# Low parts of split weights a tick later, the last weight pair two ticks later, and other ticks for the scores of the second unit, in an attention and gated feed-forward kernel

## Chip, cores and metric

The kernel runs on one core of one Trainium2 chip. The metric is device time in microseconds for one execution. Three runs of the kernel before took 1147.52, 1148.4 and 1149.6 us, with a median of 1148.4. A change of 0.2% is 2.3 us.

## What is computed

The reference does attention over 8 batches, 8 heads, 576 positions and 64 dimensions, with a window of 32 keys (heads 0 to 3) or of 128 keys of which every fourth counts (heads 4 to 7), and then a gated feed-forward layer over the 4608 resulting rows of 512 numbers:

```python
scores = scale * np.matmul(q, k.transpose(0, 1, 3, 2))
scores = np.where(masks[None], scores, -1e9)
attn = np.exp(scores - np.max(scores, axis=-1, keepdims=True))
attn = attn / (np.sum(attn, axis=-1, keepdims=True) + 1e-09)
x = (attn @ v).transpose(0, 2, 1, 3).reshape(B * S, H * D)
xn = x / np.sqrt(np.mean(x * x, axis=-1, keepdims=True) + 1e-06) * rms_g
g = xn @ w_gate
out = (g * (1 / (1 + np.exp(-g))) * (xn @ w_val)) @ w_out
```

Weights are 512 x 1536 (gate, value) and 1536 x 512 (output). They come as float64, as two 32-bit words each, and the kernel turns them into float32 itself.

## The kernel before

**Units and parts.** The rows are worked off in 16 units u of 288 rows (half a batch). A unit's attention has 14 bursts (a block of queries of two heads): each needs scores (q), four or five ticks later transposes of the normalised probabilities (t), and then outputs (o). A unit's feed-forward has 12 column blocks j of 128, each in three parts: gate (part 0), val (part 1) and proj (part 2, the output product of the block before). TensorE (PE) runs these products; the attention of unit u + 1 is woven into the feed-forward of unit u.

**Ticks.** The order of work is written out by hand in ticks. `now[0]` counts them. 25 ticks come before the main loop (attention of unit 0); then each part of each block is a tick t = 3(uN + j) + part, with N = 12 blocks (loop at L790 to L815; t = 2 is the first, as the gate and val of block 0 stand at the end of the first loop). In a tick PE gets its 8 or 12 matmuls and then, by `attend` (L752), the transposes, outputs and scores that fall into it. What the other engines have to do is put off: `later(dt, rank, fn)` (L110) files a function for the tick dt ahead, and `flush` (L113) at the start of a tick issues what is filed for it, in order of rank. Each engine works off its own queue in the order of issue, so the rank is the place in the queue. Ranks of one tick: 0 tanh on ScalarE (ACT) or prod on VectorE (V, L679), 0.2 emptying the transposes (ACT L446, from unit 2 on also V L448), 0.5 emptying outputs and splitting h (ACT L690, GpSimd (POOL) L691), 0.6 normalising x (L585, L602, L603), 0.7 the score maximum (V L361, L366), 0.8 silu (V L666), 0.9 the low part of a query (V L344), 2 the exponentials (ACT L376), -1 or 2.1 the sums and the normalisation (V L385 and L386, POOL L391 or ACT L389), 3 to 3.3 high parts of keys, queries and values (ACT), 4 adding outputs (V L421), 5 a step of weight decoding (V) or the low part of keys (POOL L335), 5.1 the low part of values (POOL L305), 6 splitting a weight, 8 to 9 the next rebase, 9.9 the next weight load (SP).

**Weights.** 36 pieces (a block of gate, val or output weights) make 18 pairs. A pair is loaded raw, rebased on ACT (`rebase`, L151, with a multiply on POOL at L162) and then decoded on V: for the pairs from the fifth on in two steps, `rest` (L176) and `whole` (L180). `step` (L208) takes the next of these from a list; if the pair is not rebased yet, it first calls `ahead` (L217), which rebases. In the main loop of unit 0 one step is filed per tick (L797); the last pair, with the output blocks 10 and 11, has its steps in ticks 31 and 32 and its rebase in tick 31. Unit 0 multiplies in full float32; from unit 1 on (t = 36) each product is made of three matmuls with high and low parts. For that, `split_weight` (L227) takes one piece per tick: at even ticks from 4 to 30, and at every tick from 37 on (L794). ACT copies the high part (L242) and V or POOL subtracts it to get the low part (L243), both at rank 6 of the same tick; POOL does it at even ticks from 38 on.

**The plan of unit 1.** `plan` (L745) files the bursts of a unit in ticks. For unit 1 the ticks are given as a list (L767), relative to t = 0; transposes follow after 5 and outputs after 7 ticks.

**Banks.** Gate and val products alternate between the PSUM banks "g" and "v": `bank` (L634) gives block j's gate and val the two in turn. Transposes in a gate or val tick go into unused columns of that tick's own bank; in a proj tick they get a tile of their own in the bank `bank("g", j)` (L812). Scores use the single bank "s" from tick 4 on (L814).

```python
                if used and (t >= SPLITS[2] or t % 2 == 0 and SPLITS[0] <= t < SPLITS[1]):
                    later(0, 6, lambda: split_weight(*used.pop(0), V if t < SPLITS[1] or t % 2 else G))
                if u == 0:
                    decode(1)
```

Of the kernel before, what the change touches and what calls it, by code (L numbers as in the profile page):

```python
# [14 lines left out]
ALU = mybir.AluOpType  # L15
# [24 lines left out]
SIGNS = 4  # L40
SPLITS = 4, 31, 37


ORDER = [(0, 0, "q"), (0, 1, "q"), (0, 0, "v"), (0, 2, "q"), (0, 0, "w"), (0, 1, "v"), (0, 3, "qv"), (0, 2, "v"),
         (0, 0, "g"), (0, 0, "w"), (0, 0, "w"), (1, 0, "qv")]
# [22 lines left out]
def attn_moe(ctx: ExitStack, tc: tile.TileContext, qk_in, v_in, w_gate, w_val, w_out, rms_g, outT):  # L68
# [41 lines left out]
    def later(dt, rank, fn):  # L110
        put_off.setdefault(now[0] + dt, []).append((rank, fn))

    def flush():  # L113
        for _, fn in sorted(put_off.pop(now[0], []), key=lambda e: e[0]):
            fn()
# [86 lines left out]
    def decode(k):  # L202

        for i in range(k):
            later(0, 5 + 2 * i, step)
        later(0, 8.9, rebase_next)
# [16 lines left out]
    def single(kind, j):  # L223
        n = pieces.index((kind, j))
        return fs[n // 2][:, n % 2]

    def split_weight(kind, j, e):  # L227
        n = pieces.index((kind, j))
        m, k = divmod(n, 2)

        tag = f"hi{n if n % 4 == 3 and n < 2 * NP - 4 else n - n % 4}"
        if tag not in his:
            parts = 1 if n % 4 == 3 and n < 2 * NP - 4 else 3 if n < 2 * NP - 4 else 4
            his[tag] = cst.tile([P, parts, NC, P], F32R, tag=tag, name=f"{tag}_{kind}{j}")
        hi = his[tag][:, 0 if tag == f"hi{n}" else n % 4]
        if k == 0:
            los[m] = cst.tile([P, 2, NC, P], F32R, tag=f"slot{state['free']}", name=f"lo_{m}")
        else:
            state["free"] = m
        lo = los[m][:, k]  # L240
        wts[kind, j] = hi, lo
        A.copy(out=hi, in_=single(kind, j))  # L242
        e.tensor_tensor(out=lo, in0=single(kind, j), in1=hi, op=ALU.subtract)  # L243


    heads, vs, late = {}, {}, []
# [387 lines left out]
    def bank(kind, j):  # L634
        return "gv"[(j + (kind == "v")) % 2]
# [62 lines left out]
    def proj(u, j):  # L698
        if u == 0:
            used.append(("o", j))  # L700
        h = hs.pop((u, j))
        for d in range(NC):
            if j == 0:
                acc[u, d] = ps.tile([P, 512], F32, tag=f"acc{d}", name=f"acc_{u}_{d}")[:, :U]
            three(acc[u, d], weight("o", u, j), d, h, j == 0, j == NJ - 1)
            if j == NJ - 1:
                later(1, 0.7, lambda d=d: give(u, d))
# [37 lines left out]
    def plan(u, base, q_at, t_at, o_at):  # L745
        for b, *ts in zip(bursts(u), q_at, t_at, o_at):
            for kind, t in zip("qto", ts):
                events.setdefault(base + t, {})[kind] = b
        events.setdefault(base + o_at[-1] + (4 if u == 1 else 3), {})["sum"] = u
        events.setdefault(base + o_at[-1] + (4, 7, 5)[min(u, 2)], {})["apply"] = u  # L750
# [12 lines left out]
    for u in range(1, NU):  # L763
        q_at = [LAST - (LAST - EARLY[u > NNAT]) * (nb - 1 - k) // (nb - 1) for k in range(nb)]
        t_at, o_at = [t + 5 for t in q_at], [t + 8 for t in q_at]
        if u < NNAT:
            q_at = (-4, -2, -1, 1, 2, 4, 5, 7, 8, 10, 11, 13, 14, 16)  # L767
            t_at, o_at = [t + 5 for t in q_at], [t + 7 for t in q_at]
        plan(u, ends - 2 + 3 * NJ * (u - 1), q_at, t_at, o_at)
    for n in range(ends):  # L770
# [19 lines left out]
    for u in range(NU):  # L790
        for j in range(NJ):
            for part in range(0 if u + j else 2, 3):
                t = 3 * (u * NJ + j) + part
                if used and (t >= SPLITS[2] or t % 2 == 0 and SPLITS[0] <= t < SPLITS[1]):  # L794
                    later(0, 6, lambda: split_weight(*used.pop(0), V if t < SPLITS[1] or t % 2 else G))
                if u == 0:
                    decode(1)  # L797
                opening = len(ops) <= 2
                flush()
                if opening and not late:  # L800
                    early.close()
                    late.append(ctx.enter_context(tc.tile_pool(name="late", bufs=2)))
                if part == 0:
                    free = gate(u, j)
                elif part == 1:
                    free = val(u, j)
                else:
                    if prev is not None:
                        proj(*prev)
                    prev = (u, j)  # L810
                    free = None
                    if "t" in events.get(now[0], {}):  # L812
                        free = ps.tile([P, 512], F32, tag=bank("g", j), name=f"t_{u}_{j}")[:, :2 * QB]
                attend(free, s_tag="acc2" if t < 4 else "s")  # L814
                now[0] += 1  # L815
# [70 lines left out]
```

## Time and profile before

| | |
|---|---|
| median of three runs | 1148.4 us |
| the profiled execution: its own time | 1148.22 us |
| its span, from the first to the last instruction | 1146.4 us |
| mean granted clock of TensorE, share of 2.4 GHz | 0.997 |
| PE busy | 1120.8 us, 98% of the span |
| V, ACT, POOL busy | 69%, 62%, 54% |
| DMA | 82.19 MB, 72 GB/s on average |

Times in the trace are microseconds from the start of the span. Engines are PE (TensorE matmuls), PEld (its weight loads), DVE (VectorE, called V in the text), ACT (ScalarE), POOL (GpSimd), SP (the queue that issues DMAs). A timeline row gives start, duration, engine, line, operation, what is written and read, how many instructions were merged (x8), and in brackets the idle time of the engine just before, with the instruction whose end released it. Since matmuls are pipelined, their durations overlap. The profile is of one execution, so sums are made against 1148.22.

### The profile page before, as it was taken

How to read it: one execution, taken by the hardware profiler on the slowest of the kernel's cores; microseconds unless marked ns; L12 is line 12 of the kernel's file. 1: busy time of each engine (PE TensorE's matmuls, PEld its weight loads, DVE VectorE, ACT ScalarE, POOL GpSimd, SP SyncE). 2: the span in 40 equal slices, each digit the busy share in tenths (PEclk: the TensorE clock that was granted, in tenths of full speed). 3: DMA queues.
4: the chain of work that ended last, by engine and by line, in shares of the span. 5: the costliest groups of instructions: out<-in, count | busy, mean ns of one | idle time of the engine just before them, and what ended most of it. 6: DMA issues, size and time to landing. Idle time of an engine off the chain costs nothing.

```text
span 1146.4 us, 25956 instructions
## 1 busy us (share of the span) xinstructions
PE 1120.8 (98%) x8357; PEld 1088.0 (95%) x8357; DVE 793.4 (69%) x2893; ACT 714.6 (62%) x2610; POOL 620.8 (54%) x1073
## 2 busy tenths in 40 slices
PE   8898888999999999999999999999999999999998
PEld 7676778999999999999999999999999999999998
DVE  7889865867767586776758677585866758586411
ACT  5686676766657576675757657576765757576311
POOL 8235576655546465564547556465655646565211
PEclk9999999999999999999999999999999999999999
DMA  9555211311212121121212213121221312120000
GB/s 246 168 202 205 89 48 38 93 50 50 83 38 82 40 84 52 52 89 33 79 41 83 58 41 94 34 86 41 71 63 45 95 27 87 41 79 15 2 21 21
DMA packets 61545, 82.19 MB, mean 72 GB/s; under 512 B 7298, under 2 KB 41090, under 8 KB 61410
## 3 DMA queue, kind: packets, MB, share of 16 engines
q1 hardware_dynamic: 61410, 80.54, 23.6%
q8 instruction: 67, 1.10, 0.4%
q14 instruction: 68, 0.56, 0.2%
HBM read 71.08 MB, written 9.44 MB: 70 GB/s over the span
## 4 chain that ended last, share of the span: by engine, by line
PE 85%; DVE 6%; ACT 4%; issue 2%; DMA 1%; POOL 1%; POOLq 0%; SPq 0%; DVEq 0%; ACTq 0%
PE acc L622 8%; PE g L622 8%; PE v L622 8%; PE acc L623 8%; PE g L624 8%; PE g L623 8%; PE acc L624 8%; PE v L623 8%; PE v L624 8%; PE s L489 3%; PE o L477 3%; PE o L478 1%; PE busy L739 1%; ACT t L376 1%; DVE lo L243 1%
## 5 line engine op out<-in xcount | busy, mean ns | idle before, releaser
L691 POOL TENSOR_TENSOR hlo<-th,hhi 128x288 fp32r<-128x288 f32 x180 | 145.2, 807 | 201.5 <-ACT hhi L690 153.7
L624 PE MATMUL acc<-hhi,lo 128*128 128x288 f32 x720 | 212.2, 295 | 0.0
L391 POOL TENSOR_SCALAR t<-t,sum 72x72 f32<-72x72 f32 (+3 forms) x414 | 154.0, 384 | 71.9 <-DVE sum L386 65.2
L624 PE MATMUL v<-xhi,lo 128*128 128x288 f32 x612 | 180.8, 295 | 0.0
L624 PE MATMUL g<-xhi,lo 128*128 128x288 f32 x612 | 180.6, 295 | 0.0
L376 ACT ACTIVATE t<-t,sum 96x128 f32<-96x128 f32 (+3 forms) x448 | 165.6, 375 | 11.7 <-DVE sum L366 11.0
L690 ACT CAST hhi<-th 128x288 fp32r<-128x288 f32 x180 | 78.1, 434 | 141.0 <-DVE th L679 138.8
L305 POOL TENSOR_TENSOR vlo<-vt,vhi 128x128 fp32r<-128x128 f32 x196 | 93.3, 476 | 109.3 <-ACT vhi L301 96.9
L421 DVE TENSOR_TENSOR xraw<-o,xraw 64x96 f32<-64x96 f32 (+1 forms) x392 | 106.8, 272 | 56.4 <-ACT xraw L411 50.4
L661 ACT ACTIVATE th<-g 128x288 f32<-128x288 f32 x180 | 73.9, 410 | 106.6 <-PE g L624 87.7
L624 PEld LDWEIGHTS acc<-hhi,lo 128*128 128x128 f32 x720 | 135.6, 188 | 0.0
L666 DVE SCALAR_TENSOR_TENSOR th<-th,g 128x288 f32<-128x288 f32 x180 | 80.4, 447 | 69.4 <-ACT th L661 69.4
L624 PEld LDWEIGHTS v<-xhi,lo 128*128 128x128 f32 x612 | 115.3, 188 | 0.0
L624 PEld LDWEIGHTS g<-xhi,lo 128*128 128x128 f32 x612 | 115.0, 188 | 0.0
L622 PE MATMUL g<-xhi,hi_g 128*128 128x288 f32 x357 | 110.7, 310 | 1.6 <-DVE sum L385 0.9
L335 POOL TENSOR_TENSOR ks<-qk,ks 128x288 fp32r<-128x288 f32 (+2 forms) x112 | 111.0, 1005 | 0.0
L622 PE MATMUL acc<-hhi,hi_o 128*128 128x288 f32 x360 | 110.8, 308 | 0.0
L411 ACT COPY xraw<-o 64x96 f32<-64x96 f32 (+1 forms) x392 | 101.5, 259 | 12.5 <-PE o L478 10.1
L679 DVE TENSOR_TENSOR th<-th,v 128x288 f32<-128x288 f32 x180 | 81.5, 453 | 38.1 <-PE v L624 30.0
L623 PE MATMUL acc<-hlo,hi_o 128*128 128x288 f32 x360 | 106.9, 297 | 0.0
L361 DVE TENSOR_TENSOR t<-s,mask 96x256 f32<-96x256 f32 (+3 forms) x196 | 71.5, 365 | 50.9 <-PE s L489 45.7
L623 PE MATMUL g<-xlo,hi_g 128*128 128x288 f32 x322 | 94.8, 294 | 0.0
(184 smaller groups left out, 3581.2 us busy)
## 6 DMA issues: line engine op xcount, KB each, us to landing
qk<-in_qk_dram SPq DMA_DIRECT2D x60, 288.0 KB, 2.8
vt<-in_v_dram SPq DMA_DIRECT2D x196, 64.0 KB, 1.9
qk<-in_qk_dram SPq DMA_DIRECT2D x30, 352.0 KB, 3.0
out_dram<-ot SPq DMA_DIRECT2D x64, 144.0 KB, 1.9
qk<-in_qk_dram SPq DMA_DIRECT2D x30, 304.0 KB, 2.8
raw<-in_w_gate_dram SPq DMA_DIRECT2D x12, 512.0 KB, 4.7
raw<-in_w_val_dram SPq DMA_DIRECT2D x12, 512.0 KB, 5.3
raw<-in_w_out_dram SPq DMA_DIRECT2D x12, 512.0 KB, 4.3
```

Source lines behind the costliest of these rows:

```text
L305: G.tensor_tensor(out=vl, in0=vs.pop(b), in1=vh, op=ALU.subtract)
L335: ek.tensor_tensor(out=ks[:, 1, :nkt], in0=kr, in1=ks[:, 0, :nkt], op=ALU.subtract)
L376: A.activation(out=t[:nq, a, :n], in_=t[:nq, a, :n], func=AF.Exp, scale=-1.0, bias=sm[:nq, a, 0:1], accum_out=sm[:nq, a, 1:2] if u else None)
L391: (V if u == 0 and (c, i) > (NC - 1, 0) else G).tensor_scalar(out=t[:nq, a, :n], in0=t[:nq, a, :n], scalar1=sm[:nq, a, 3:4], scalar2=1.0, ...
L411: A.copy(out=to[a * D:(a + 1) * D], in_=o[a * D:(a + 1) * D, (2 + a) * nq:(3 + a) * nq])
L421: V.tensor_tensor(out=to[rows], in0=o[rows, a * nq:(a + 1) * nq], in1=to[rows], op=ALU.add)
L622: PE.matmul(out, wh[:, cc, :], xh, start=start, stop=False)
L623: PE.matmul(out, wh[:, cc, :], xl, start=False, stop=False)
L624: PE.matmul(out, wl[:, cc, :], xh, start=False, stop=stop)
L666: V.scalar_tensor_tensor(out=t, in0=t, scalar=1.0, in1=g, op0=ALU.add, op1=ALU.mult)
L679: V.tensor_tensor(out=t, in0=t, in1=v_ps[:, :U], op=ALU.mult)
L691: G.tensor_tensor(out=lo, in0=t, in1=hi, op=ALU.subtract)
```

## The change

Three things change. The low part of a split weight is filed one tick later, at rank 3.4, instead of being issued right behind its high part. In ticks 31 and 32 no decode step is filed; at the end of tick 32 (rank 8.9) the rebase of the last pair is filed, and its two steps fall into ticks 33 and 34. The scores of unit 1 that were at ticks 5, 8, 11 and 14 go to 6, 9, 12 and 15, with the transposes five and the outputs seven ticks behind them.

```diff
--- before.py
+++ after.py
@@ -40,6 +40,7 @@
 SIGNS = 4
 SPLITS = 4, 31, 37
 
+PAUSE = 31, 32
 
@@ -240,7 +241,7 @@
         lo = los[m][:, k]
         wts[kind, j] = hi, lo
         A.copy(out=hi, in_=single(kind, j))
-        e.tensor_tensor(out=lo, in0=single(kind, j), in1=hi, op=ALU.subtract)
+        later(1, 3.4, lambda: e.tensor_tensor(out=lo, in0=single(kind, j), in1=hi, op=ALU.subtract))
 
@@ -764,7 +765,7 @@
         q_at = [LAST - (LAST - EARLY[u > NNAT]) * (nb - 1 - k) // (nb - 1) for k in range(nb)]
         t_at, o_at = [t + 5 for t in q_at], [t + 8 for t in q_at]
         if u < NNAT:
-            q_at = (-4, -2, -1, 1, 2, 4, 5, 7, 8, 10, 11, 13, 14, 16)
+            q_at = (-4, -2, -1, 1, 2, 4, 6, 7, 9, 10, 12, 13, 15, 16)
             t_at, o_at = [t + 5 for t in q_at], [t + 7 for t in q_at]
         plan(u, ends - 2 + 3 * NJ * (u - 1), q_at, t_at, o_at)
@@ -794,7 +795,9 @@
                 if used and (t >= SPLITS[2] or t % 2 == 0 and SPLITS[0] <= t < SPLITS[1]):
                     later(0, 6, lambda: split_weight(*used.pop(0), V if t < SPLITS[1] or t % 2 else G))
                 if u == 0:
-                    decode(1)
+                    decode(t not in PAUSE)
+                    if t == PAUSE[-1]:
+                        later(0, 8.9, ahead)
                 opening = len(ops) <= 2
                 flush()
                 if opening and not late:
```

## Rows read from the trace of the kernel before

**Rows 1.** Stretches: start:end, length, busy us of each engine (instructions), PEclk, DMA share, GB/s

```profile
36.00:88.00 52.00, 48.08 (x247) 38.21 (x246) 43.71 (x126) 42.05 (x134) 14.42 (x10) 0.97 0.52 183
88.00:130.00 42.00, 37.02 (x162) 27.70 (x160) 39.17 (x61) 23.75 (x60) 22.01 (x20) 1.00 0.44 154
130.00:190.00 60.00, 50.62 (x364) 48.13 (x364) 42.69 (x160) 43.58 (x152) 42.80 (x64) 0.97 0.21 60
190.00:1146.40 956.40, 952.18 (x7406) 948.20 (x7404) 641.79 (x2426) 583.42 (x2189) 513.27 (x918) 1.00 0.19 56
```

**Rows 2.** Timeline of PE, ticks 5, 6 and 8

```profile
48.54 0.49 PE L472 MATMUL o<-pt,v 128*128 128x192 f32 x2
51.85 0.58 PE L486 MATMUL s<-qk 128*72 128x104 f32 x4 [2.83 <-DVE sum L366]
52.27 3.81 PE L619 MATMUL g<-xn,f 128*128 128x288 f32 x8
...
58.90 2.13 PE L619 MATMUL acc<-h,f 128*128 128x288 f32 x8
```

**Rows 3.** Stretches of 2 us, columns as in rows 1

```profile
52.00:54.00 2.00, 2.00 (x8) 1.56 (x8) 2.00 (x7) 1.84 (x4) 0.00 (x0) 0.58 0.96 389
...
148.00:150.00 2.00, 2.00 (x12) 1.98 (x11) 0.89 (x4) 1.67 (x6) 2.00 (x4) 0.50 0.04 8
150.00:152.00 2.00, 2.00 (x13) 2.00 (x12) 1.58 (x4) 0.81 (x3) 1.07 (x3) 0.67 0.00 1
```

**Rows 4.** Timeline of DVE, end of tick 4 and start of tick 5

```profile
48.59 1.29 DVE L172 SCALAR_TENSOR_TENSOR f<-raw,f 128x1024 uint32<-128x1024 uint32 x1
50.33 0.69 DVE L243 TENSOR_TENSOR lo<-f,hi_g 128x512 fp32r<-128x512 f32 x1 [0.45 <-ACT hi_g L242]
50.94 0.45 DVE L679 TENSOR_TENSOR h<-h,v 128x288 f32<-128x288 f32 x1
```

**Rows 5.** Timeline of ACT, the same place

```profile
49.70 0.60 ACT L242 CAST hi_g<-f 128x512 fp32r<-128x512 f32 x1
51.42 0.32 ACT L446 COPY pt<-v 128x192 f32<-128x192 f32 x1 [1.12 <-DVE h L679]
```

**Rows 6.** Timeline of PE, ticks 18 to 57: rows with idle time, and proj(10)

```profile
84.17 2.21 PE L619 MATMUL g<-xn,f 128*128 128x288 f32 x8 [0.50 <-ACT pt L446]
...
99.13 2.21 PE L619 MATMUL g<-xn,f 128*128 128x288 f32 x8 [0.44 <-DVE h L679]
...
106.74 2.21 PE L619 MATMUL g<-xn,f 128*128 128x288 f32 x8 [1.52 <-DVE h L679]
...
113.86 2.21 PE L619 MATMUL g<-xn,f 128*128 128x288 f32 x8 [0.50 <-DVE h L679]
...
122.24 2.21 PE L619 MATMUL g<-xn,f 128*128 128x288 f32 x8 [1.23 <-DVE h L679]
...
126.84 2.10 PE L619 MATMUL acc<-h,f 128*128 128x288 f32 x8
...
129.79 0.37 PE L622 MATMUL g<-xhi,hi_g 128*128 128x288 f32 x1 [0.68 <-ACT pt L446]
...
147.04 0.40 PE L622 MATMUL v<-xhi,hi_o 128*128 128x288 f32 x1 [1.78 <-DVE pt L448]
...
183.58 0.37 PE L622 MATMUL g<-xhi,hi_g 128*128 128x288 f32 x1 [0.86 <-DVE sum L385]
```

**Rows 7.** Timeline of DVE, ticks 22, 31, 35 and 41

```profile
97.41 1.29 DVE L243 TENSOR_TENSOR lo<-f,hi_g 128x512 fp32r<-128x512 f32 x1
...
120.02 1.80 DVE L177 SCALAR_TENSOR_TENSOR raw<-raw 128x1024 uint32<-128x1024 uint32 x1 [0.82 <-POOL raw L162]
...
129.24 0.45 DVE L679 TENSOR_TENSOR h<-h,v 128x288 f32<-128x288 f32 x1
...
145.64 0.69 DVE L243 TENSOR_TENSOR lo<-f,hi_o 128x512 fp32r<-128x512 f32 x1 [1.16 <-POOL vlo L305]
```

**Rows 8.** Timeline of POOL, while V made a low part at 97.41

```profile
96.38 1.78 POOL L335 TENSOR_TENSOR ks<-qk,ks 128x288 fp32r<-128x288 f32 x1
```

## The prediction

> **What bounds the kernel now.** I read the stretch table first, then the PE timeline with its idle times, then the VectorE (V) and ScalarE (ACT) timelines before each idle time. "Tick t" is step 3j+part of the main loop; the change touches ticks 4 to 59.
>
> The stretch table [rows 1] says where time can be had. From 190 us to the end PE is busy 952.18 of 956.40 us: nothing is left there, so whatever is gained or lost before 190 us arrives at the end unchanged, for PE simply starts its full stretch earlier or later. Before that, PE leaves 52.00 - 48.08 = 3.9 us (36 to 88), 42.00 - 37.02 = 5.0 us (88 to 130) and 60.00 - 50.62 = 9.4 us (130 to 190) idle, and the granted clock is 0.97 in the first and the last of these. V is busy 39.17 of 42.00 us between 88 and 130: there it is nearly as full as it can be.
>
> The largest single hole is at tick 5 [rows 2]. PE finishes the outputs behind proj(0) at 49.03 (48.54 + 0.49) and waits 2.83 us for V's score maximum before it may write tick 5's scores at 51.85, because ticks 4 and 5 share the one bank "s". Then the gate matmuls of tick 6 take 3.81 us where the same eight took 2.13 at tick 8: the granted clock is 0.58 from 52 to 54 [rows 3], so they ran mostly at 1.2 GHz instead of 2.4, after PE had stood still.
>
> V's timeline tells why the maximum is late [rows 4]. The sign step of tick 4 ends at 49.88. Then comes tick 4's low part (L243), which cannot start before ScalarE has made the high part, at 49.70 + 0.60 = 50.30 [rows 5]; V stands 0.45 us, subtracts for 0.69, and only then runs prod(1) (L679, 50.94) and the maximum. ACT in turn waits for prod(1) before it empties the transposes at 51.42. So a result that PE needs 14 ticks later (piece n is split at tick 23+n and used at 37+n, for n from 14) stands ahead of work that PE needs at once.
>
> **The change part by part.**
>
> 1. *Low parts a tick later, rank 3.4.* Nothing is added or removed: 14 low parts on V (even ticks 4 to 30), 11 on V and 11 on POOL (ticks 37 to 58). Each now stands behind the next tick's prod, maximum, silu and query low part, on POOL also behind the normalisation and hlo, and ahead of that tick's add and decode step. Its high part is then long done, so the wait for ACT goes too; no DMA hangs on it.
>
> At tick 5: sign ends 49.88, prod(1) takes 0.45 and ends about 50.3; ACT, free of the high part at 50.30, copies the transposes in 0.32, to 50.6; gate(2) can start at 50.7, against 52.27. That is 1.57 us, less 0.42 for the score matmuls that now come at tick 6 (52.27 - 51.85): **1.15**. The clock price of that hole is 3.81 - 2.13 = 1.68. What is left of the hole is 50.7 - 49.03 = 1.67 us; PE kept 2.4 GHz after 1.52 us of idle at 106.74 [rows 6] and lost it after 1.78 us at 147.04 [rows 3, 6]. 1.67 lies between, so I take half, **0.85**, and keep 0 and 1.68 as ends.
>
> At ticks 18 and 24 PE waits 0.50 and 0.44 us [rows 6], for the emptied transposes behind prod(5) and for prod(7); each of these stands behind a low part, the second behind one of 1.29 us at 97.41 [rows 7]. I take both: **0.9**, ends 0 and 0.94. At tick 27 the wait is 1.52 us, for prod(8); V had no idle time worth a row there and the same work stands before prod(8) as before, only in another order: **0**, upper end 1.52. At tick 30 the 0.50 us wait for prod(9) follows a low part directly: **0.5**, lower end 0, since the factor for the second unit's normalisation, which passes ACT and POOL, is due in the same tick.
>
> In ticks 37 to 59 V's low part of tick 41 waits 1.16 us and then takes 0.69 [rows 7] (the row names POOL's low value part; by the code L243 waits for ACT's high part); behind it is the low half of the transposes that PE waits for 1.78 us at 147.04, and the granted clock is 0.50 from 148 to 150 and 0.67 to 152 [rows 3, 6]. With the low part out of the way that copy comes 0.7 us earlier, about 1.1 us of hole is left, which is less than the 1.52 after which the clock stayed up: 0.7 plus the clock's price. By the clock column that price is half of 2 us plus a third of 2 us, 1.67. Together 2.4. At tick 57 the wait of 0.86 us [rows 6] is for a sum that also stands behind a low part: 0.7. The other stalls of this stretch are waits for copies and adds in front of which the low part stays (rank 3.4 is ahead of the add's 4); I give them 0.6. Sum **3.7**; the ends are 0.7 (only one low part's own length) and 7 (three quarters of the 9.4 us).
>
> 2. *The last pair two ticks later.* Before, its rest step (1.80 us at 120.02, and V stood 0.82 before it for POOL's sign multiply, which follows ACT's rebase) runs ahead of prod(10), and PE waits 1.23 us for prod(10) at 122.24 [rows 6, 7]. Now ticks 31 and 32 have no decode step, and rebase and multiply go to the end of tick 32, past ACT's copies and POOL's xlo and ks of that tick. prod(10) can follow silu: **+1.23**. The pair issues no load (all 18 pairs are loaded). But proj(10) at tick 35 reads this very pair. Before, V worked on without a pause from the rest step to prod(11), which began at 129.24 [rows 7]; now the pair's last step is the last thing ahead of prod(11), so it ends near 129.24 - 0.82 = 128.4 if every step keeps its length, and near 127.4 if the two long steps take half a microsecond less each, as the step of the same size at 48.59 did with its 1.29 us [rows 4]. proj(10) began at 126.84 [rows 6]; without its earlier stall PE asks for the pair at 126.84 - 1.23 = 125.6. I take 127.4, a new wait of 127.4 - 125.6 = **-1.8** at tick 35; ends 0 and -2.8. The 0.68 us at tick 36 [rows 6], a wait for prod(11), is then past before PE comes there: **+0.68**. Net 0.1, ends -0.9 and 1.9.
>
> 3. *Scores of unit 1 at other ticks.* No matmul more or less: moved are tick 5's to 6, 8's to 9, 11's to 12, 14's to 15, with transposes five and outputs seven ticks behind; the last of each stays. On SP one load (64 KB, the third unit's second value block) is issued a tick later, at 23, and the first such block is split on ACT and POOL at tick 33 instead of 32; its first use is at tick 38, so both cost nothing. Pairs of ticks remain (6 and 7, 9 and 10, and so on), but the second of a pair is now a val tick, in whose V queue no prod stands ahead of the maximum. Transposes move from val ticks into proj ticks (11, 14, 17, 20), where they have a bank of their own and ACT need not wait for prod. I count **0** beyond tick 5; what hides the moved work is PE's two microseconds of matmuls per tick.
>
> Sum: 1.15 + 0.85 + 0.9 + 0 + 0.5 + 3.7 + 0.1 = 7.2 us. The profiled execution took 1148.22, which becomes 1141.0; it stands 0.2 under the median of 1148.4, so against that median **1141.2**. The lower ends make 1.15 + 0 + 0 + 0 + 0 + 0.7 - 0.9 = 0.95 (1147.4), the upper ones 1.15 + 1.68 + 0.94 + 1.52 + 0.5 + 7 + 1.9 = 14.7 (1133.7).
>
> **The rivals.**
>
> *VectorE is the bound, and swallows it.* V has 2.8 us to spare in 88 to 130 [rows 1] and none of its work goes. Then what is won at tick 5 is lost again by tick 27, the last pair's shift gives nothing, and only 0.7 of the last stretch is left: 1147.5. For it: the 1.52 us at tick 27. Against it: V idles before many low parts, and that idle time goes. 0.11.
>
> *The low parts run into POOL.* A low part took 0.69 us at 50.33 and 1.29 at 97.41, where POOL's ks at 96.38 needed 1.78 [rows 4, 7, 8]. In the middle of a tick a low part may meet POOL's work more often. If every second of the 25 on V took the longer time, V had 12 times 0.6, 7.2 us, more to do, and where that stood on the path the whole gain of 7.2 would be gone: 1148.4. I hold it for unlikely, since the low parts at the end of a tick met POOL too: 0.05. The Trainium skill's GPSIMD Engine Reference, section 1, Specifications, says that POOL shares its SBUF interfaces with VectorE and that they contend for VectorE instructions with two SBUF inputs, which L243 is; the two times agree with that, though neither isolates it.
>
> *Slower: proj(10) waits for the last pair.* Where V stays behind as in the first rival, the pair ends at the late end, 2.8 us after PE asked, and a hole of that size cost the clock too at tick 5 (1.68). With the stall of 1.23 gone and nothing else won, 2.8 + 1.68 - 1.23 = 3.25 us worse: 1151.6. It decides once the pair's last step ends more than 1.23 us after PE asks and V has won nothing before. For it: V's full stretch ahead of it. Against it: the tick before has no decode step. 0.06.
>
> *Most holes close.* If V's and ACT's mutual waits resolve so that the upper ends hold, 1134 to 1136, say 1135. 0.12.
>
> That the change does not do what it says is possible for the scores alone: the pair of ticks 4 and 5 becomes 6 and 7, and the wait might come back there. It would then take back the 1.15 us and the 0.85 of part 1: 1143.2, inside the range.
>
> **How the numbers follow.** A change of this kernel can be told from none from about 0.2%, 2.3 us. Forecast 0.66, most holes 0.12: faster 0.78. V the bound 0.11 and POOL 0.05: same 0.16. The proj(10) wait: slower 0.06. The range takes the forecast's bounds, the first rival and most of the closing holes, 1135.0 to 1147.5; outside lie the slower case, POOL's, and some of the best.
>
> **What would show it.** Right: at tick 5 idle under 1.8 us and prod(1) directly behind the sign step; no idle on V before L243; no clock fall near 148; the wait at 122 gone and a wait of about 1.8 us before proj(10); from there to the end the same duration as before. Wrong: V without idle and PE's idle in 88 to 130 unchanged; low parts on V of 1.2 us as a rule; a hole over 2.8 us before proj(10); or a new wait for the maximum at ticks 7, 10, 13, 16.

## The result and the profile after

The changed kernel took 1150.61 us (median of 20 runs, 1149.34 to 1153.36), the kernel before 1148.81 us (20 runs beside them, 1146.6 to 1150.6). The ratio is 1.0017 with a 95% interval of 1.0010 to 1.0024: about 2 us slower, where 7.2 us less were forecast. The profiled execution took 1150.23 us, with a span of 1148.4.

The same four stretches as in [rows 1], of the changed kernel, with the same columns:

```profile
36.00:88.00 52.00, 49.42 (x256) 39.15 (x254) 46.07 (x131) 43.72 (x139) 14.76 (x10) 1.00 0.56 190
88.00:130.00 42.00, 34.48 (x138) 26.47 (x139) 37.47 (x57) 22.20 (x54) 20.71 (x20) 0.91 0.44 148
130.00:190.00 60.00, 51.04 (x356) 48.12 (x355) 45.07 (x155) 42.39 (x148) 39.87 (x62) 0.95 0.18 53
190.00:1148.40 958.40, 954.63 (x7423) 950.68 (x7421) 644.11 (x2431) 584.73 (x2194) 515.48 (x919) 1.00 0.20 56
```

The first stretch gained (PE busy 49.42 instead of 48.08 us, clock 1.00 instead of 0.97). The second lost: 34.48 us busy, at a clock of 0.91 instead of 1.00. In the third PE is busy for 51.04 us, but at 0.95, so part of that is only slower work.

PE's timeline of the changed kernel, the places that answer to [rows 2, 6] (ticks 5 and 6, 20, 27, 35, 43, 46):

```profile
47.99 0.49 PE L473 MATMUL o<-pt,v 128*128 128x192 f32 x2
50.14 2.21 PE L620 MATMUL g<-xn,f 128*128 128x288 f32 x8 [1.66 <-ACT pt L447]
...
89.64 0.51 PE L473 MATMUL o<-pt,v 104*128 104x144 f32 x2 [1.68 <-ACT xraw L409]
...
104.70 3.21 PE L620 MATMUL g<-xn,f 128*128 128x288 f32 x8 [2.23 <-DVE h L680]
...
128.97 3.58 PE L620 MATMUL acc<-h,f 128*128 128x288 f32 x8 [3.65 <-DVE f L182]
...
148.76 0.40 PE L623 MATMUL v<-xhi,hi_o 128*128 128x288 f32 x1 [1.07 <-DVE pt L449]
...
156.62 0.40 PE L623 MATMUL v<-xhi,hi_g 128*128 128x288 f32 x1 [1.73 <-DVE pt L449]
```

The hole of 2.83 us at tick 5 is 1.66, that of 1.78 at 147.04 is 1.07, and the wait of 1.23 before the gate at 122.24 is gone. In their place stand a hole of 1.68 at tick 20, 2.23 instead of 1.52 at tick 27, 3.65 before proj(10) and 1.73 at tick 46. Stretches of 2 us of the changed kernel (columns as in [rows 3]) show what followed three of them:

```profile
106.00:108.00 2.00, 2.00 (x7) 1.38 (x6) 1.88 (x3) 1.25 (x2) 0.20 (x1) 0.50 0.03 12
...
130.00:132.00 2.00, 2.00 (x6) 1.41 (x5) 0.74 (x6) 0.00 (x0) 0.72 (x2) 0.50 0.02 4
...
158.00:160.00 2.00, 2.00 (x10) 1.94 (x10) 1.89 (x9) 0.00 (x0) 0.90 (x2) 0.50 0.20 32
```

From the starts of the ticks (first gate, val or proj matmul) in both traces, one execution of each kernel, changed kernel minus kernel before; negative is earlier. The forecast column puts the terms of the prediction at their places:

| between the starts of ticks | forecast, us | measured, us |
|---|---|---|
| 3 and 9 | -2.0 (1.15 + 0.85) | -2.77 |
| 9 and 26 | -0.9 | +0.57 |
| 26 and 30 | -0.5 | +3.40 |
| 30 and 34 | -1.23 | -1.96 |
| 34 and 37 | +1.12 (1.8 - 0.68) | +4.31 |
| 37 and 66 | -3.7 | -0.66 |

Tick 3 itself began 0.55 earlier, and the rest after tick 66 was 0.34 shorter (946.20 against 945.86): -0.55 + 2.89 - 0.34 = +2.00, the difference of the spans.

### The profile page after: what moved, and what is told of

The parts are those of the page before. It is cut to its first block, busy times and chain, and to the rows that moved or that the text cites. A ratio compares the mean times of both kernels' runs of the same rounds, so it can differ in the third digit from the quotient of the medians.

```text
span 1148.4 us, 25939 instructions
## 1 busy us (share of the span) xinstructions
PE 1122.5 (98%) x8357; PEld 1090.3 (95%) x8357; DVE 799.0 (70%) x2893; ACT 714.8 (62%) x2610; POOL 619.1 (54%) x1073
## 4 chain that ended last, share of the span: by engine, by line
PE 87%; DVE 5%; ACT 5%; issue 1%; POOL 1%; DMA 1%; POOLq 0%; SPq 0%; ACTq 0%
PE v L623 9%; PE acc L623 9%; PE g L623 8%; PE acc L624 8%; PE v L624 8%; PE v L625 8%; PE g L625 8%; PE g L624 8%; PE acc L625 8%; PE s L490 3%; PE o L478 3%; PE o L479 1%; PE busy L740 1%; ACT t L377 1%; PE v L464 1%
```

## The experiments

Each kernel was timed beside the kernel before, on one chip for those that came together (the first four; the next four; the next four; the last two). The chips' own times differ, so ratios are compared and not medians. The full stretch after tick 66 differed by up to 4.7 us between single executions (945.74 to 950.39), so causes are read ahead of it. A profiled execution need not be a typical one: kernel 4's was the slowest of its 11 (1150.94 us, median 1147.76), kernel 6's the fastest of its 12 (1144.79, median 1147.53), and kernel 1's was 1.85 us above its median. The table gives how far each profiled execution stands behind the kernel before at the start of ticks 26, 31, 37 and 66; the changed kernel is the first row.

| kernel | ratio, 95% interval | t26 | t31 | t37 | t66 |
|---|---|---|---|---|---|
| the change | 1.0017 (1.0010 to 1.0024) | -2.75 | +0.19 | +3.00 | +2.34 |
| 1 low parts alone | 0.9989 (0.9981 to 0.9998) | -3.57 | +1.35 | +1.51 | +0.91 |
| 2 scores alone | 1.0004 (0.9995 to 1.0013) | +0.56 | +0.19 | +0.07 | +0.09 |
| 3 last pair alone | 1.0040 (1.0028 to 1.0052) | -0.47 | -0.79 | +3.43 | +3.42 |
| 4 low parts and scores | 1.0001 (0.9992 to 1.0010) | -2.66 | +0.48 | +0.49 | +2.02 |
| 5 = 4, one decode step later | 0.9990 (0.9981 to 0.9999) | -2.67 | -1.96 | -1.89 | -2.46 |
| 6 = 4, PE filled at tick 26 | 0.9982 (0.9972 to 0.9991) | -2.66 | -1.94 | -1.87 | -2.93 |
| 7 = 4, pair one tick later | 0.9983 (0.9973 to 0.9992) | -0.95 | -1.74 | -2.73 | -3.34 |
| 8 = 4, late low parts as before | 1.0010 (1.0002 to 1.0019) | -2.77 | +0.11 | +0.14 | +0.13 |
| 9 = 4, other bank at tick 20 | 0.9997 (0.9987 to 1.0007) | -2.92 | -1.15 | -1.15 | +0.40 |
| 10 the change, pair ahead of queries | 0.9994 (0.9985 to 1.0002) | -2.79 | -1.24 | -0.20 | -0.75 |
| 11 low parts, pair one tick, filled | 0.9969 (0.9957 to 0.9981) | -4.21 | -3.13 | -4.12 | -2.68 |
| 12 = 11 with the scores | 0.9984 (0.9975 to 0.9993) | -2.74 | -1.90 | -2.89 | -1.48 |
| 13 the change, rebase in tick 31 | 1.0010 (1.0000 to 1.0019) | -2.80 | -2.35 | -0.31 | +1.25 |
| 14 = 3, rebase in tick 31 | 1.0020 (1.0007 to 1.0033) | -0.01 | -0.40 | +1.94 | +1.84 |

### The parts alone (1 to 4)

Low parts alone:

```diff
-        e.tensor_tensor(out=lo, in0=single(kind, j), in1=hi, op=ALU.subtract)
+        later(1, 3.4, lambda: e.tensor_tensor(out=lo, in0=single(kind, j), in1=hi, op=ALU.subtract))
```

> Only the low parts move. Theory 'the last pair' (the loss is the wait of proj(10) for the pair that comes two ticks later, 3.65 us plus a clock fall, and the low parts themselves are a gain): faster than before by 1 to 4 us, ratio 0.9965 to 0.999, the hole at tick 5 shorter than 2.8 us. Theory 'the clock at tick 27' (what PE gains early turns into a longer hole at tick 27, behind a full VectorE, and the clock falls there): no faster than before by more than 0.5 us, a hole over 1.8 us at tick 27 with the granted clock at half behind it.

0.9989. Between ticks 26 and 31 it loses 4.92 us (from -3.57 to +1.35): the hole at tick 27 is 2.88 us and the granted clock 0.50 in every 2 us from 104 to 114. What was won by tick 26 is given back there in this execution. The time, 0.0011 less than before, is what the first theory expects; the hole and the clock are what the second does.

Scores alone:

```diff
-            q_at = (-4, -2, -1, 1, 2, 4, 5, 7, 8, 10, 11, 13, 14, 16)
+            q_at = (-4, -2, -1, 1, 2, 4, 6, 7, 9, 10, 12, 13, 15, 16)
```

> Only the scores of unit 1 move. 'The last pair': the hole at tick 5 shrinks (the score no longer waits there), perhaps the clock does not fall there; 0 to 2 us faster. 'The clock at tick 27': the same as before within 0.5 us, whatever is won at tick 5 is lost by tick 28.

No difference that can be told. PE's timeline of this kernel, ticks 6 and 20:

```profile
51.98 3.55 PE L619 MATMUL g<-xn,f 128*128 128x288 f32 x8 [2.77 <-ACT pt L446]
...
92.63 0.51 PE L472 MATMUL o<-pt,v 104*128 104x144 f32 x2 [1.33 <-ACT xraw L408]
```

Without the scores of tick 5 the hole stays, now ahead of the gate, for the copied transposes wait for prod(1) behind the low part. So it is the low part that holds tick 5 (kernel 1, with the scores as before, has only 1.68 us there); and the hole at tick 20 is there with the scores alone.

The last pair alone:

```diff
+PAUSE = 31, 32
...
-                    decode(1)
+                    decode(t not in PAUSE)
+                    if t == PAUSE[-1]:
+                        later(0, 8.9, ahead)
```

> Only the last pair moves two ticks. 'The last pair': slower than before by 1.5 to 3 us (wait of 1.8 to 3.7 us before proj(10), less the 1.23 us at tick 33, plus a clock fall). 'The clock at tick 27': within 1 us of before, as everything up to tick 30 is unchanged.

1.0040 in five executions, 4.1 us between the medians (1152.39 and 1148.27): this part by itself makes the kernel slower, more than the whole change does. PE, V and ACT in its trace, one row or two of each engine's timeline:

```profile
128.83 4.21 PE L620 MATMUL acc<-h,f 128*128 128x288 f32 x8 [4.50 <-DVE f L182]
```
```profile
120.98 1.18 DVE L604 TENSOR_TENSOR xlo<-xraw,xhi 128x288 fp32r<-128x288 f32 x1 [1.16 <-ACT xhi L603]
```
```profile
119.49 1.14 ACT L160 ACTIVATE f<-raw 128x1024 f32<-128x1024 f32 x1
120.52 0.43 ACT L603 CAST xhi<-xraw 128x288 fp32r<-128x288 f32 x1
```

The hole is 4.50 us and proj(10) then runs at half the clock (4.21 us against 2.10 in [rows 6]). Ahead of it V stands 1.16 us for the high part of the normalised x, which ACT makes behind the moved rebase.

Low parts and scores together (the edits of 1 and 2):

> Low parts and scores move, the last pair stays. 'The last pair': faster than before by 0.8 us or more (1148.0 or less against 1148.8), since the waits at ticks 33 and 36 come back (1.9 us) but the wait of 3.65 us and the clock fall of 0.7 us go. 'The clock at tick 27': still slower than or equal to before, with a hole over 1.8 us at tick 27 and 3 us lost to the clock behind it.

1.0001: the whole change without its second part is no slower than before, and 0.0016 better than with it (the two intervals just touch). It is not faster than before either, as the second theory has it: by tick 31 its early gain is gone in the profiled execution (from -2.66 to +0.48).

### Tick 27 (5 and 6)

Kernel 4 with the decode step of tick 25 done in tick 27, beside that tick's own:

```diff
-                    decode(1)
+                    decode({25: 0, 27: 2}.get(t, 1))
```

> Low parts and scores moved, the last pair as before, and one decode step taken out of tick 25 and made up in tick 27, so that no step of 1.2 to 2.1 us stands ahead of prod(8) on VectorE. Theory 'full VectorE and the clock': the hole of 2.44 us at tick 27 shrinks to under 1 us and the clock does not fall behind it; 3 to 5 us faster than low_scores (1147.8), so 1143 to 1145. Rival 'the hole just moves': VectorE is full until tick 30, the next prod is late instead, at most 1 us faster than low_scores.

Kernel 4 with eight matmuls of ones into the idle bank "s" between proj(7), the product of tick 26, and the gate of tick 27:

```diff
+                if t == 26:
+                    fill_ps = ps.tile([P, 512], F32, tag="s", name="fill")
+                    for _ in range(8):
+                        PE.matmul(fill_ps, ones, ones[:, None, :].to_broadcast([P, 4, P]), start=True, stop=True)
```

> As low_scores, with eight matmuls of ones (128x512, into the free scores bank) in PE's queue between proj(8) of tick 26 and the gate of tick 27; they change no result. They take 1.8 us of a hole of 2.44. 'Full VectorE and the clock': the granted clock stays at full behind the hole and 3 us come back, 1144 to 1146 against 1147.8 for low_scores. Rival (the clock's fall costs nothing, since VectorE sets the pace there): within 0.7 us of low_scores.

PE of kernel 5, then PE of kernel 6 and its stretch from 106 to 108:

```profile
110.69 2.21 PE L619 MATMUL g<-xn,f 128*128 128x288 f32 x8 [1.29 <-DVE h L679]
114.53 0.40 PE L571 MATMUL bps<-rd,ones 96*128 96x288 f32 x1 [1.30 <-ACT rd L555]
```
```profile
102.18 2.21 PE L818 MATMUL fill<-ones 128*128 128x512 f32 x8
105.05 2.21 PE L619 MATMUL g<-xn,f 128*128 128x288 f32 x8 [0.65 <-DVE h L679]
```
```profile
106.00:108.00 2.00, 2.00 (x14) 1.66 (x13) 2.00 (x3) 1.46 (x3) 0.12 (x1) 1.00 0.16 60
```

Kernel 6 waits for prod(8) as long as kernel 4 (its gate starts at 105.05, kernel 4's at 104.99), but does work while it waits, and the clock stays at 1.00: from the gate of tick 27 to tick 29 it takes 4.52 us (105.05 to 109.57) where kernel 4 took 7.88 (104.99 to 112.87). In these two executions 3.4 us are the price of the clock alone. The times give less: 1.0001 against 0.9982 is about 2.2 us, on two chips. The mean granted clock of all executions agrees with that: it is 0.9965 over the 11 of kernel 4, none above 0.997, and 0.9986 over the 12 of kernel 6, seven of them at 0.999 or 1.0; the difference of 0.0021 is 2.4 us of the span, an estimate. Kernel 5 takes the wait away instead (tick 27 starts at 102.78); it is 5.57 us ahead of kernel 4 at tick 29 but only 2.44 at tick 31, since 1.29 and 1.30 us of waiting, for prod(9) and for the factor of the normalisation, come up behind it. Both are at the same place by tick 31, and their intervals overlap: that removing the wait is worth more here than keeping the clock through it is not shown. Kernel 5's own gain on kernel 4, 0.0011 with intervals that overlap, is nearer to the rival 'the hole just moves' than to the 3 to 5 us of the theory.

### The late low parts (8)

Kernel 4 with the low parts from tick 37 on where they stood before:

```diff
-        later(1, 3.4, lambda: e.tensor_tensor(out=lo, in0=single(kind, j), in1=hi, op=ALU.subtract))
+        if now[0] < ends + 35:
+            later(1, 3.4, lambda: e.tensor_tensor(out=lo, in0=single(kind, j), in1=hi, op=ALU.subtract))
+        else:
+            e.tensor_tensor(out=lo, in0=single(kind, j), in1=hi, op=ALU.subtract)
```

> As low_scores, but the low parts of ticks 37 to 59 stand where they stood before. If the low parts in the middle of these ticks win 0.7 us and a clock fall, as predicted: 2 to 4 us slower than low_scores (1150 to 1152). If they only move the holes (1.76 us at tick 46 for the 1.78 at tick 43): within 1 us of low_scores.

1.0010 against kernel 4's 1.0001 on another chip: by the times the late low parts are worth about 0.001, 1 us, with intervals that overlap. The table shows no steady gain between ticks 37 and 66. The four kernels without these moves (2, 3, 8, 14) need the time of the kernel before there, within 0.1 us. Of the eleven rows with them, six are 0.55 to 1.06 us shorter (the change, 1, 5, 6, 7, 10) and five 1.41 to 1.56 us longer (4, 9, 11, 12, 13); in each of these five the granted clock fell to 0.50 between 172 and 185 us, and in none of the six at that place. Kernel 3 had a fall there too, from 174 to 178, without losing time, so that the fall is the whole cause of these losses is not shown. PE at tick 43 and a stretch of kernel 8:

```profile
147.19 0.40 PE L625 MATMUL v<-xhi,hi_o 128*128 128x288 f32 x1 [1.79 <-DVE pt L451]
```
```profile
148.00:150.00 2.00, 2.00 (x18) 2.00 (x18) 0.88 (x5) 1.83 (x8) 2.00 (x4) 1.00 0.03 8
```

The hole is the one of before (1.78 in [rows 6]), and yet the clock stayed at 1.00, where it was 0.50 in [rows 3]. Kernel 8 is only 0.6 us faster from tick 41 to 45 than the kernel before for it (+0.15 to -0.44).

### The last pair (7, 10, 13, 14)

Kernel 4 with the pair one tick later instead of two:

```diff
-                    decode(1)
+                    decode(t != 31)
+                    if t == 31:
+                        later(0, 8.9, ahead)
```

> Low parts and scores moved, the last pair one tick later only (no step in tick 31, rebase at its end, rest in 32, whole in 33). 'The place in VectorE's queue': the hole before proj(10) is under 1 us instead of 3.65, and the waits at ticks 33 and 36 of low_scores (1.40 and 0.68) go or shrink: 0.5 to 2 us faster than low_scores, and 3 us faster than the changed kernel. Rival (any later pair makes PE wait): a hole of 1.5 us or more before proj(10), no faster than low_scores.

0.9983: the hole before proj(10) is 0.95 us and the wait at tick 33 is gone as well; from tick 31 to 37 it gains 0.99 where the change loses 2.81.

The changed kernel with the pair's last step in tick 34 ahead of the query's low part (rank 0.85 instead of 5):

```diff
-                    decode(t not in PAUSE)
+                    if t == 34:
+                        later(0, 0.85, step)
+                    else:
+                        decode(t not in PAUSE)
```

> The changed kernel with the last pair's second step ahead of the query's low part in tick 34 (rank 0.85 instead of 5). 'The place in VectorE's queue': the hole of 3.65 us before proj(10) shrinks by about the 1.5 us that this low part took, to 2.1 us; 1 to 2.5 us faster than the changed kernel. Rival (the pair waits for rebase or for its first step, not for its place): hole of 3.2 us or more, within 0.5 us.

The hole is 1.86 us, half of 3.65, and the ratio 0.9994. V of this kernel, then PE:

```profile
124.47 1.21 DVE L182 SCALAR_TENSOR_TENSOR f<-f,raw 128x1024 uint32<-128x1024 uint32 x1
125.71 1.50 DVE L345 TENSOR_TENSOR qs<-qk,qs 64x288 fp32r<-64x288 f32 x1
```
```profile
125.74 3.90 PE L620 MATMUL acc<-h,f 128*128 128x288 f32 x8 [1.86 <-DVE f L182]
```

The changed kernel, and kernel 3, with only the rebase back at the end of tick 31:

```diff
-                    if t == PAUSE[-1]:
+                    if t == PAUSE[0]:
                         later(0, 8.9, ahead)
```

> The changed kernel with the rebase of the last pair filed at the end of tick 31, where the kernel before has it, instead of tick 32; the two decode steps stay in ticks 33 and 34. Theory (the moved rebase holds ScalarE's high part of the normalised x of tick 33, and VectorE waits for that): in the changed kernel the rebase at 119.62 took 1.15 us and that high part began at 120.68, 0.27 us later than 0.54 us behind its input; VectorE then stood 0.33 us and its low part of x, beside GpSimd's multiply of the rebase, took 1.17 us instead of 0.45. Without both the pair ends up to 1.05 us earlier, and the hole before proj(10) goes from 3.65 to 2.6 to 3.0 us; time 1 to 2 us below the changed kernel, a ratio to the kernel before of about 1.0002 to 1.0010. Rival (only the length of VectorE's queue between silu(10) and the pair's last step counts): the hole stays within 0.3 us of 3.65 and the ratio at 1.0017.

> The kernel before with the last pair's two steps in ticks 33 and 34, its rebase left at the end of tick 31, and nothing else. With the rebase in tick 32 VectorE stood 1.16 us for ScalarE's high part (begun at 120.52, its input at hand from 119.43 on) and its low part of x took 1.18 us. Theory: without that the pair ends 1.1 to 1.8 us earlier, the hole of 4.50 us before proj(10) becomes 2.7 to 3.4 us, and the ratio falls from 1.0040 to between 1.0015 and 1.0030. Rival (the queue's length alone): the hole stays at 4.2 us or more and the ratio at 1.003 to 1.005.

PE and V of kernel 13, then PE of kernel 14:

```profile
125.73 3.81 PE L620 MATMUL acc<-h,f 128*128 128x288 f32 x8 [2.95 <-DVE f L182]
```
```profile
118.35 0.56 DVE L604 TENSOR_TENSOR xlo<-xraw,xhi 128x288 fp32r<-128x288 f32 x1 [0.33 <-ACT xhi L603]
```
```profile
128.15 3.60 PE L620 MATMUL acc<-h,f 128*128 128x288 f32 x8 [3.44 <-DVE f L182]
```

The holes are 0.70 and 1.06 us shorter, as expected of the theory for kernel 13 and a little less than that for kernel 14. The ratio of kernel 14 is half of kernel 3's loss (1.0020 against 1.0040, intervals that overlap a little); that of kernel 13 lies at the upper end of the expected range, and its interval overlaps the change's. V's wait of 0.33 us for the high part did not go in kernel 13, since copies for keys and queries stand ahead of it on ACT, so the wait that the theory names gave none of the 0.70: the low part of x is 0.6 us shorter there, away from GpSimd's multiply, and the weight's low part before it took 0.68 instead of 0.92. In kernel 14 both parts came: the wait fell from 1.16 to 0.51 us and the low part of x from 1.18 to 0.78. That it is the multiply which lengthens a step is not shown; in kernel 13 that same weight's low part, at 116.12, ran beside it (116.36 to 117.83) without being longer.

### The scores again (9, 11, 12)

Kernel 4 with the outputs of tick 20 in bank "s":

```diff
-                attend(free, s_tag="acc2" if t < 4 else "s")
+                attend(free, s_tag="acc2" if t < 4 else "s", o_tag="s" if t == 20 else "o")
```

> As low_scores, but the outputs of tick 20 go to the scores bank, which is free by then, instead of the one outputs bank. Theory 'the scores part gives its gain back at tick 20' (outputs of ticks 19 and 20 now follow each other, and the second must wait until ACT, behind a rebase, has emptied the first): the hole of 1.70 us before the outputs of tick 20 goes to under 0.4 us, and 0 to 1.5 us are won, less what the hole at tick 27 takes back. Rival (ACT is late for everything there): the hole appears at tick 21 or 22 instead with the same length.

The hole in front of the outputs of tick 20 goes, and 0.90 us of it comes back at once ahead of the next gate. Tick 21 starts 0.72 us earlier than in kernel 4 and tick 26 only 0.26; the ratios of the two kernels (0.9997 and 1.0001) can't be told apart. PE of this kernel:

```profile
89.35 2.21 PE L619 MATMUL g<-xn,f 128*128 128x288 f32 x8 [0.90 <-DVE h L679]
```

Low parts (1), pair one tick later (7) and the filling matmuls (6), with the scores as before, and the same with the scores of the change:

> Candidate for the best: low parts moved, scores as before, last pair one tick later, eight matmuls of ones in the hole of tick 27. If the three gains stand side by side (0.9 of the low parts, 2.2 of the matmuls, 2.1 of the one tick, in us against their references): 0.9955 to 0.997 of before. Rival (the factor of the second unit's normalisation sets the start of tick 31 whatever comes before): 0.998 or more.

> The same with the scores moved too. If the scores part gives its gain back at tick 20: 0 to 1.5 us slower than low_one_fill. If it helps once the rest is mended: faster by 0.5 us or more.

Kernel 11 is the fastest of all, 0.9969 (0.9957 to 0.9981), and beats both kernels; with the scores it is 1.5 us slower (medians 1146.39 of ten executions and 1144.91 of five, on the same chip). Kernels 1 and 4 differ by nearly as much in their ratios (0.9989 and 1.0001). The intervals overlap in both pairs. The same two stretches of kernel 11:

```profile
88.00:130.00 42.00, 38.83 (x181) 30.76 (x182) 38.79 (x71) 22.52 (x59) 25.40 (x24) 1.00 0.42 141
130.00:190.00 60.00, 50.39 (x353) 47.88 (x352) 44.38 (x146) 42.67 (x149) 41.35 (x63) 0.94 0.19 55
```

From 88 to 130 the clock is whole. In the last stretch it still falls in this execution (0.50 from 174 to 178), after holes of 1.0 to 1.4 us; kernel 7, with the same holes, kept its clock there.

## Why the prediction was wrong

**Where the forecast was missed.** By the ratios, the low parts alone won 0.0011, 1.3 us (kernel 1), where their terms add up to 7.1; the scores took back 1.4 us (kernel 4 against kernel 1) for a term of 0; the last pair cost 1.8 us (the change against kernel 4) for a gain of 0.1. The last two differences are about as large as their intervals. The low parts are the largest miss; the last pair is what makes the kernel slower than before. The clock runs through all three. Its mean is 0.9953 over the 20 executions of the changed kernel and 0.9976 over the 111 of the kernel before that ran beside the experiments. On that difference the change loses 2.7 us, an estimate, where the forecast counted on winning 2.5 (0.85 and 1.67).

**The last pair: the step that turned a gain into a loss.** The prediction took a net of 0.1 us, with a new wait of 1.8 at tick 35 and an end of 2.8, and no price for the clock in it, although 1.8 lies above the 1.78 after which its own rows show the clock fall. The gain at tick 33 came (1.96 between ticks 30 and 34, forecast 1.23), the 0.68 at tick 36 went as said, and PE asked at 128.97 - 3.65 = 125.3, forecast 125.6. What failed is the step from V's old stretch to its new end: that between silu(10) and prod(11) V has the same work as before, less its pause and the shorter long steps. The pair was ready at 128.9 and not at 127.4. V of the changed kernel, ticks 32 to 35, and then ACT:

```profile
118.30 0.45 DVE L667 SCALAR_TENSOR_TENSOR h<-h,g 128x288 f32<-128x288 f32 x1
118.66 0.92 DVE L244 TENSOR_TENSOR lo<-f,hi_v 128x512 fp32r<-128x512 f32 x1
119.50 0.44 DVE L680 TENSOR_TENSOR h<-h,v 128x288 f32<-128x288 f32 x1
119.87 0.93 DVE L586 SCALAR_TENSOR_TENSOR xraw<-xraw,gs,bps 128x288 f32<-128x288 f32 x2
121.13 1.17 DVE L604 TENSOR_TENSOR xlo<-xraw,xhi 128x288 fp32r<-128x288 f32 x1 [0.33 <-ACT xhi L603]
...
124.11 1.23 DVE L178 SCALAR_TENSOR_TENSOR raw<-raw 128x1024 uint32<-128x1024 uint32 x1
...
125.98 1.53 DVE L345 TENSOR_TENSOR qs<-qk,qs 64x288 fp32r<-64x288 f32 x1
127.55 1.36 DVE L182 SCALAR_TENSOR_TENSOR f<-f,raw 128x1024 uint32<-128x1024 uint32 x1
128.84 0.44 DVE L680 TENSOR_TENSOR h<-h,v 128x288 f32<-128x288 f32 x1
```
```profile
119.62 1.15 ACT L160 ACTIVATE f<-raw 128x1024 f32<-128x1024 f32 x1
120.68 0.42 ACT L603 CAST xhi<-xraw 128x288 fp32r<-128x288 f32 x1
```

From silu(10) at 118.30 to prod(11) at 128.84 it is 10.54 us; before it was 10.49 (118.75 to 129.24). The forecast took 1.8 off this (0.82 of waiting, 1.0 of shorter steps), and both went. But 1.9 came back. A low part that part 1 had itself moved from ahead of silu to behind it takes 0.84 (118.66 to 119.50). V waits 0.33 for the high part of x, and the low part of x takes 0.72 more (1.17 instead of 0.45), beside GpSimd's multiply for the rebase. The prediction named the queues that the rebase is moved past, and did not ask for whom the rebase would then stand in the way. Kernels 13 and 14 show what its place costs: 0.70 and 1.06 us of the hole, in kernel 13 without the wait of 0.33.

The loss between ticks 34 and 37 is 4.31 us and not 1.12. Of the 3.2 us between them 1.85 is the longer hole (3.65 for 1.8) and the rest the price of the clock: the hole left proj(10) at 1.2 GHz (3.58 us instead of 2.10). This was the rival "Slower: proj(10) waits for the last pair", with its place and the clock behind the hole right, at a chance of 0.06. That its time came out near (3.25 us slower, measured about 2) is in part luck: it had the pair late because long steps keep their length, and these got shorter while other work filled their place; and it took nothing as won before. The point from which it decides, an end more than 1.23 us after PE asks, was already passed in the forecast's own 1.8; it held the rival down only by gains elsewhere that didn't last.

**Tick 27: a term of 0, and +3.4 us from tick 26 to 30 in the profiled execution.** The prediction saw that V's work before prod(8) stays the same. It did not draw the consequence: if PE comes earlier by more than V does, the hole grows by the difference. PE began tick 26 2.75 us earlier and the gate behind prod(8) 2.04, so the hole grew by 0.71. V of the changed kernel:

```profile
101.57 0.69 DVE L244 TENSOR_TENSOR lo<-f,hi_g 128x512 fp32r<-128x512 f32 x1
102.18 2.10 DVE L178 SCALAR_TENSOR_TENSOR raw<-raw 128x1024 uint32<-128x1024 uint32 x1
104.20 0.44 DVE L680 TENSOR_TENSOR h<-h,v 128x288 f32<-128x288 f32 x1
```

There is no idle time here; V sets the place of the gate, as in the rival "VectorE is the bound", though most of the gain still came through. What took the rest is the clock: it fell behind this hole of 2.23 us, as it had not behind 1.52, and by tick 30 another 2.69 us were gone, where kernels 6 and 9, with their clock whole, each win 0.66. The length of the hole does not decide it alone. Of the six kernels with nothing in the hole and 2.17 to 2.88 us of it, five lost the clock behind it (the change, 1, 4, 8 and 10), and kernel 9 kept it with 2.84; the three that fill it (6, 11, 12) all kept it, as did kernel 13 with 1.55. PE of kernel 9 and its stretch:

```profile
105.13 2.21 PE L619 MATMUL g<-xn,f 128*128 128x288 f32 x8 [2.84 <-DVE h L679]
```
```profile
88.00:130.00 42.00, 34.78 (x157) 26.45 (x155) 38.91 (x64) 22.88 (x57) 23.54 (x20) 1.00 0.43 142
```

Why the clock fell behind one of these holes and not behind the other stays open.

**The late low parts: 3.7 forecast, 0.66 won in the profiled execution and about 1 by the times (kernel 8).** At tick 43 all came as said: hole 1.07 for the forecast 1.1, no fall, 2.75 us won from tick 41 to 45 (forecast 2.4). One tick later 1.95 of it were gone. V of the changed kernel, ticks 45 and 46:

```profile
152.41 0.36 DVE L449 TENSOR_TENSOR pt<-v,pt 128x192 fp32r<-128x192 f32 x1 [0.93 <-ACT pt L447]
...
153.44 1.89 DVE L345 TENSOR_TENSOR qs<-qk,qs 64x288 fp32r<-64x288 f32 x1
155.35 0.69 DVE L244 TENSOR_TENSOR lo<-f,hi_g 128x512 fp32r<-128x512 f32 x1
...
156.23 0.33 DVE L449 TENSOR_TENSOR pt<-t,pt 128x192 fp32r<-128x192 f32 x1
```

The copy that PE needs stands behind a query's low part of 1.89 us and the moved low part. Where the low part was out of the way of one copy it got in the way of another. And V's work grew: by the groups of lines from 130 to 190 us, queries and the low parts of value weights of the changed kernel,

```profile
L345 DVE TENSOR_TENSOR qs<-qk,qs 64x288 fp32r<-64x288 f32 x6 | 7.1, 1183 | 0.2
L244 DVE TENSOR_TENSOR lo<-f,hi_v 128x512 fp32r<-128x512 f32 x3 | 5.0, 1657 | 1.1 <-POOL lo L244 1.1
```

against 5.0 us (842 ns each) and 2.1 us (689 ns) before. The other low parts on V got a little shorter (5.9 us for 6.7), so all 11 took 10.9 us instead of 8.8. This is the mechanism of the rival "The low parts run into POOL": one low part took 3.35 us, at 168.58, while GpSimd ran four instructions from 168.99 on without a pause. How much of it reached PE is not shown. Nor did the gain hold in every execution: five of eleven traces lose about 1.5 us in this stretch, with a clock fall near its end. The Trainium skill's GPSIMD Engine Reference, section 1, Specifications, has POOL share its SBUF interfaces with VectorE and contend with its instructions of two SBUF inputs; the trace agrees, with 3.35 against 0.69 us for the same instruction, though no run isolates it.

**The scores: 0 forecast, about 1.5 us lost beside the moved low parts, nothing that can be told alone (kernel 2).** The prediction followed the banks of scores and transposes but not that of the outputs. The outputs of ticks 19 and 20 now follow each other in the one bank "o", and ACT empties it only after a rebase: ACT of the changed kernel,

```profile
88.00 1.12 ACT L160 ACTIVATE f<-raw 128x1024 f32<-128x1024 f32 x1
89.02 0.56 ACT L409 COPY xraw<-o 64x72 f32<-64x72 f32 x2
```

Kernel 9 moved the outputs to another bank and got 0.72 us of the hole of 1.70 back by the next tick. So the bank makes the hole; V, late for the next prod, takes the rest. That the hole is also what the scores cost in time is not shown, as kernel 9 is not clearly faster than kernel 4. Taking the rebase out of ACT's way at this place was not tried. The prediction's fear for the scores themselves, a return of the wait at ticks 6 and 7, did not come true.

**What was right.** Tick 5: 1.67 us of hole forecast, 1.66 measured, prod(1) directly behind the sign step, and no fall of the clock there (1.00 from 36 to 88), so that the other half of its price came back as well (2.77 us won from tick 3 to 9, forecast 2.0). The stretch from tick 66 to the end kept its length in these two executions, within 0.34 us. That V was nearly full from 88 to 130 was read; it was given a chance of 0.11 and should have been in every term behind tick 9, since where V has no idle time a part of the gain ahead goes into the next hole. Two slips of the working change nothing in it: the first rival's 1147.5 is counted from the profiled execution and not from the median, and the low part of tick 4 is first used at tick 36, 32 ticks later and not 14.

## What to carry to other kernels

Work that is moved out of the way of one consumer on an in-order queue stands in the way of the next: before a gain is counted, go to the next place where PE waits for that engine, and if the engine has no idle time in between, carry a part of the gain over as a longer hole there and reckon with the clock that such a hole cost elsewhere in the trace. When a step moves, price what it now stands ahead of on each queue as well as what it waits behind. Where a wait can't be taken away, matmuls without any use in it can be worth as much as moving it away (0.9982 against 0.9990 here, with intervals that overlap).

## What had not been expected

- The clock stayed at 1.2 GHz long after the hole, with PE busy throughout: 6.8 us after the hole at tick 27 in the changed kernel, 10.2 us in kernel 1 (0.7 of it still within the hole), against some 3.3 us after the hole at 147.04 (2.0 and, at 0.67, another 1.3 by the clock column of [rows 3]). One hole of 2.88 us so cost kernel 1 nearly 5 us by tick 31, its own growth of 1.36 us included.
- Holes of the same length did not do the same: 1.78 us lost the clock in the kernel before, 1.79 at the same place did not in kernel 8; 2.88 at tick 27 did in kernel 1, 2.84 there did not in kernel 9; 1.68 at tick 20 did not in the changed kernel, 1.74 there did in kernel 7, whose clock was 0.50 from 92 to 94 (and its t26 is only -0.95 for it). The forecast's choice of one half for 1.67 us was as much as could be had from lengths.
- The price read from the clock column can overstate: 1.67 us by [rows 3], yet kernel 8, which kept the clock at tick 43, was only 0.6 us ahead at tick 45, after a wait of 0.76 us for the next copy.
